# PSUM banks given out oldest free first instead of lowest free first

## The chip, the cores and the metric

The kernel runs on one core of one Trainium2 chip. The core has a matrix engine (TensorE, PE in the profile), a vector engine (DVE), a scalar engine (ACT), GpSimd (POOL) and a sync engine (SP) that issues the DMAs. Matmuls write to PSUM, which is handed out here as eight banks of 128 partitions by 512 float32; DVE and ACT read them out. The metric is the device time of one execution in microseconds (us).

## What is computed

Two stages follow each other, with four batches, twelve heads, 448 tokens and a head size of 64. The first is attention that mixes heads before and after the softmax, the second a feed-forward network with a low-rank mix of the tokens ahead of it:

```python
scores = scale * np.matmul(q, k.transpose(0, 1, 3, 2))
scores = np.einsum('bhij,hg->bgij', scores, w_pre)
scores = scores - np.max(scores, axis=-1, keepdims=True)
attn = np.exp(scores)
attn = attn / (np.sum(attn, axis=-1, keepdims=True) + 1e-09)
attn = np.einsum('bhij,hg->bgij', attn, w_post)
out = np.matmul(attn, v)                     # (4, 12, 448, 64)
x = out.transpose(0, 2, 1, 3).reshape(4, 448, 768)
h = x.transpose(0, 2, 1) @ U @ V             # U 448x32, V 32x448
u = x + h.transpose(0, 2, 1)
ch = np.maximum(u @ w_ch1, 0.0) @ w_ch2      # 768 -> 3072 -> 768
return u + ch
```

## The kernel before

The program is written as a list of steps with ranks (`plan.add`), and a planner (`Plan.order`, L146) walks a model of the engines' times and writes the steps down in the order in which they would start. Each engine then runs its own steps strictly in that order. A step that needs a PSUM bank (`bank`, through `plan.where`) takes it when the planner starts it, and the bank is free again when the planner's model has finished the last step that reads it. Which bank it gets is decided by `Plan.find` (L112) and kept by `Plan.take` (L131).

The eight banks are not eight tiles. They are four tiles of two banks each, `bank0` to `bank3`, and a step that needs one bank gets half of a tile:

```python
BANKS = [sb["ps"].tile([128, 2, 512], F32, f"bank{i}") for i in range(4)]

def bank(*s):
    w = plan.where[s]
    return BANKS[w[0] // 2] if len(w) == 2 else BANKS[w[0] // 2][:, w[0] % 2]
```

The waits between engines are derived from these tiles when the program is built: an instruction that reads or writes a tile waits for earlier accesses by other engines to the same tile, whichever half they touch. Banks 2p and 2p+1 are the halves of tile `bankp`.

In attention the steps `qk` (scores, matmuls of L390), `pre` (first head mix, L421) and `post` (second head mix, L454) take a whole tile each; `av` (L492) takes one half. They are read out by copies (L302 on ACT, L304 on DVE), by the maximum (DVE, L426) and by the exponential (ACT, L431).

From about 400 us on the banks are taken one at a time. `lr` is the low-rank mix (L665, L683, L696). `up` (L736) is the product with the first weight matrix: 18 matmuls of 448 columns for one block f of 128 hidden features (24 blocks) and one batch b; `hh` (ACT, L741) and `hl` (DVE, L745) read its bank and write relu in two float32r parts. `dn` (L756) is the product with the second matrix: for one batch and one of six output columns c it is 3 matmuls per block, nearly always for two blocks at once and so 6 matmuls; `ac` (DVE, L760) adds its bank to the accumulator `acc`. At most three banks are out for `up`, six for `dn`, four for `lr`. For two blocks f and four batches that is 8 `up` and 24 `dn`, 288 matmuls; this pattern repeats 12 times. Between them DVE, POOL and ACT turn the weights from 64-bit words to float32 pairs (L580 to L601, then L302, L306, L309).

`find` gives a step of `PAIRS` (`qk`, `pre`, `post`) the lowest free tile. A step that needs one bank gets the lowest bank whose other half is taken, or else the first half of the lowest free tile.

Of the kernel before, what the change touches and what calls it, by code (L numbers as in the profile page):

```python
# [43 lines left out]
class Unit:  # L44


    def __init__(self, b, gi):
        self.b, self.gi, self.n = b, gi, UNITS[b][gi]
        self.i0 = MC * sum(UNITS[b][:gi])
        self.rows = MC * self.n  # L50
        self.tokens = min(S, self.i0 + self.rows) - self.i0
# [11 lines left out]
PAIRS = ("qk", "pre", "post")  # L63
# [23 lines left out]
class Plan:  # L87
# [8 lines left out]
    def __init__(self, rings, banked, banks, weight):  # L96
        self.left = dict(rings)
        self.banked, self.where = banked, {}
        self.bank_free = [True] * banks
        self.weight = weight  # L100
        self.steps = {}
        self.port = {}
        self.users = {}
# [7 lines left out]

    def find(self, name, free):  # L112

        pairs = [p for p in range(len(free) // 2) if free[2 * p] and free[2 * p + 1]]
        if name in PAIRS:
            return [2 * pairs[0], 2 * pairs[0] + 1] if pairs else None
        odd = [i for i, f in enumerate(free) if f and not free[i ^ 1]]
        one = odd or [2 * p for p in pairs]
        return one[:1] or None

    def fits(self, names):
        free = list(self.bank_free)
        for n in sorted(names, key=lambda n: n not in PAIRS):
            got = self.find(n, free)
            if got is None:
                return False
            for g in got:
                free[g] = False
        return True

    def take(self, s):  # L131
        got = self.find(s[0], self.bank_free)
        for g in got:
            self.bank_free[g] = False
        self.where[s] = got

    def order(self):
# [3 lines left out]
        for k, s in steps.items():  # L141
            for n in s[3]:
                assert n in steps, (k, n)
                after.setdefault(n, []).append(k)
        held, left = set(), dict(self.left)
        free = {e: 0 for e in ("SP", "PE", "ACT", "DVE", "POOL", None)}  # L146
        ready = {e: [] for e in free}
        events, seq, now, wire, out, shared = [], 0, 0, 0, [], 0

        def push(k, t):  # L150
            nonlocal seq
            seq += 1
            heapq.heappush(events, (t, seq, k, False))
# [27 lines left out]
        while events:  # L181
            now = events[0][0]
            while events and events[0][0] <= now:
                _, n, k, done = heapq.heappop(events)
                if k is None:
                    continue
                if not done:
                    for e, _ in steps[k][0]:
                        r = ready[e]
                        item = (steps[k][2], n, k)  # L190
                        i = len(r)
                        while i and r[i - 1] > item:
                            i -= 1
                        r.insert(i, item)
                    continue
                for s in steps[k][4]:
                    users[s] -= 1
                    if users[s] == 0:
                        held.discard(s)
                        if s[0] in self.banked:  # L200
                            for g in self.where[s]:
                                self.bank_free[g] = True
                        left[s[0]] += 1
                for a in after.get(k, []):
                    wait[a] -= 1
                    if wait[a] == 0:
                        push(a, now + (self.PE_LATENCY - self.LATENCY if steps[a][0][0][0] == "PE" else 0))
            moved = True
            while moved:
                moved = False  # L210
                for e in free:
                    if free[e] > now:
                        continue
                    r = pick(e)
                    if r is None:
                        continue
                    k = r[2]
                    engines, fn, _, _, slots = steps[k]
                    for o, _ in engines:
                        ready[o].remove(r)  # L220
                    for s in sorted(slots, key=lambda s: s[0] not in PAIRS):
                        if s not in held:
                            held.add(s)
                            if s[0] in self.banked:
                                self.take(s)
                            left[s[0]] -= 1
                    cost = dict(engines)[e]
                    if e == "SP":
                        cost, bytes_time = cost
                    if e == "PE" and now - free[e] > 600:  # L230
                        cost += min(cost, 850)
                    if e in self.port[k]:
                        cost += max(0, shared - now)
                        shared = now + cost
                    out.append((k, e, now, now + cost))
                    seq += 1
                    if e is None:
                        late = 0
                    else:
                        free[e] = now + cost  # L240
                        late = self.PE_LATENCY if e == "PE" else self.LATENCY
                        if e == "SP":
                            wire = max(wire, now + cost + self.DMA_START) + bytes_time
                            late = wire + self.DMA_DONE - now - cost
                        heapq.heappush(events, (now + cost, seq, None, False))
                        seq += 1
                    heapq.heappush(events, (now + cost + late, seq, k, True))
                    moved = True
# [4 lines left out]
def build(tc, q2, kt, vj, wpre_in, wpost_in, u_in, v_in, ident, w1j, w2, out, show=None):  # L253
# [305 lines left out]
    def piece(key, src, n, p, rank, finish, slots, opened, cost, early=None):  # L559
# [61 lines left out]
        if early:  # L621
            plan.add((key, "put"), [("SP", (480, 900 * s))], put, r0, [(key, 4)], [first_tmp])
            plan.add((key, "take"), [("SP", (480, 900 * s))], take, rank - RANK["raw"], [(key, "put"), opened], [tmp])
# [183 lines left out]
    if show is not None:  # L807
        show.extend(order)
# [65 lines left out]
```

## Time and profile before

| what | value |
|---|---|
| time, median of 3 runs | 1421.88 us (1420.87 to 1424.16) |
| the profiled execution | 1414.63 us |
| its span, first to last instruction | 1412.8 us |
| PE busy | 1132.8 us (80%) |
| PE weight loads busy | 891.2 us (63%) |
| DVE busy | 706.5 us (50%) |
| ACT busy | 388.0 us (27%) |
| POOL busy | 255.6 us (18%) |
| mean granted TensorE clock | 0.978 |

A busy PE is not a PE at its peak: matmuls overlap, and one of 448 columns shows as 0.36 us while the next starts 0.20 us after it. Idle time of PE is time in which no matmul is in flight. The chain of waits is the work that ended last, followed backwards; a line of it names what the end of the program was waiting for at that time. The granted clock is 1.00 at 2.4 GHz and 0.50 at 1.2 GHz.

### The profile page before, as it was taken

What the parts mean: (1) busy time and instruction counts of PE and PEld (TensorE: products, weight loads), DVE (VectorE), ACT (ScalarE), POOL (GpSimd) and SP (SyncE); (2) the same over time, 40 slices, a digit from 0 to 9 for tenths busy, and PEclk for the clock granted to TensorE, in tenths of its full rate; (3) what the DMA queues carried; (4) which work ended last, traced back from release to release, by engine and by line L of the source; (5) the groups of instructions that cost most, each with busy time, mean ns of one, the idle gap of its engine ahead of it and who ended that gap; (6) DMA issues with size and microseconds to landing.
All of it is one profiled execution on the core that took longest, in us unless ns stands there. A gap on an engine that the chain in (4) does not pass through costs nothing.

```text
span 1412.8 us, 29240 instructions
## 1 busy us (share of the span) xinstructions
PE 1132.8 (80%) x12456; PEld 891.2 (63%) x12456; DVE 706.5 (50%) x1271; ACT 388.0 (27%) x817; POOL 255.6 (18%) x389
## 2 busy tenths in 40 slices
PE   3998998988867778777787878787878877777776
PEld 0565665665655667666666666666666666666665
DVE  0654554566666457545555454454554454444433
ACT  2766566766632222110111111110111110110000
POOL 2111111121323113211121111111121111112000
PEclk8999999999988999999999999999999999999999
DMA  7566555566551002111111111111111111111013
GB/s 241 181 199 181 163 174 169 178 187 194 176 162 34 0 23 63 50 45 45 45 45 34 34 45 34 34 45 45 45 45 34 34 45 34 34 45 45 1 46 111
DMA packets 68030, 118.18 MB, mean 84 GB/s; under 512 B 17804, under 2 KB 54108, under 8 KB 67420
## 3 DMA queue, kind: packets, MB, share of 16 engines
q1 hardware_dynamic: 67900, 116.31, 27.5%
q8 instruction: 98, 1.61, 0.5%
q14 instruction: 32, 0.26, 0.1%
HBM read 62.72 MB, written 12.28 MB: 53 GB/s over the span
## 4 chain that ended last, share of the span: by engine, by line
PE 71%; DVE 15%; issue 4%; ACT 4%; DMA 4%; SPq 1%; POOL 0%; DVEq 0%; ACTq 0%; POOLq 0%
PE bank L736 26%; PE bank L756 25%; DVE acc L760 7%; PE bank L492 5%; PE bank L454 5%; PE bank L421 4%; PE bank L390 4%; DMA t<-s 3%; DVE hl L745 3%; ACT hh L741 2%; PE bank L683 1%; DVE xl L309 1%; SPq L397 1%; ACT s L302 1%; DVE acc L699 1%
## 5 line engine op out<-in xcount | busy, mean ns | idle before, releaser
L756 PE MATMUL bank<-hh,w1l 128*128 128x448 f32 x576 | 226.1, 392 | 125.6 <-DVE acc L760 75.2
L760 DVE TENSOR_TENSOR acc<-acc,bank 128x448 f32<-128x448 f32 x300 | 181.5, 618 | 246.4 <-PE bank L756 126.1
L736 PE MATMUL bank<-uh,w0l 128*128 128x448 f32 x576 | 218.4, 379 | 64.7 <-DVE hl L745 31.1
L756 PEld LDWEIGHTS bank<-hh,w1l 128*128 128x128 f32 x576 | 108.1, 188 | 186.1 <-DVE acc L760 114.6
L741 ACT ACTIVATE hh<-bank 128x448 fp32r<-128x448 f32 x96 | 52.2, 544 | 622.2 <-PE bank L736 537.9
L736 PE MATMUL bank<-ul,w0h 128*128 128x448 f32 x576 | 211.0, 366 | 0.0
L736 PE MATMUL bank<-uh,w0h 128*128 128x448 f32 x576 | 210.7, 366 | 0.0
L756 PE MATMUL bank<-hh,w1h 128*128 128x448 f32 x576 | 210.6, 366 | 0.0
L756 PE MATMUL bank<-hl,w1h 128*128 128x448 f32 x576 | 210.4, 365 | 0.0
L601 POOL TENSOR_TENSOR a<-a,x 128x384 f32<-128x384 f32 (+2 forms) x99 | 99.9, 1009 | 462.4 <-DVE x L597 455.2
L736 PEld LDWEIGHTS bank<-uh,w0l 128*128 128x128 f32 x576 | 109.0, 189 | 97.3 <-DVE hl L745 37.7
L745 DVE SCALAR_TENSOR_TENSOR hl<-bank,hh 128x448 fp32r<-128x448 f32 x96 | 59.8, 622 | 217.2 <-ACT hh L741 210.1
L426 DVE TENSOR_REDUCE mx<-bank 128x2 f32<-128x896 f32 x90 | 97.6, 1086 | 112.7 <-PE bank L421 112.7
L454 PEld LDWEIGHTS bank<-wr,e 60*56 60x56 f32 (+1 forms) x5760 | 103.0, 133 | 66.6 <-issue 59.3
L454 PE MATMUL bank<-wr,e 60*56 60x60 f32 (+1 forms) x5760 | 107.9, 220 | 26.4 <-issue 22.8
L390 PE MATMUL bank<-k,q 64*60 64x448 f32 (+1 forms) x768 | 101.4, 580 | 24.8 <-ACT s L302 18.3
L431 ACT ACTIVATE e<-bank,mx 128x448 f32<-128x448 f32 x180 | 112.7, 636 | 21.2 <-DVE rc L438 13.4
L736 PEld LDWEIGHTS bank<-uh,w0h 128*128 128x128 f32 x576 | 108.9, 189 | 8.4
L736 PEld LDWEIGHTS bank<-ul,w0h 128*128 128x128 f32 x576 | 109.2, 190 | 7.4
L756 PEld LDWEIGHTS bank<-hh,w1h 128*128 128x128 f32 x576 | 108.2, 188 | 8.8
L756 PEld LDWEIGHTS bank<-hl,w1h 128*128 128x128 f32 x576 | 108.5, 188 | 6.5
L421 PE MATMUL bank<-t,wpre 64*64 64x448 f32 x720 | 92.0, 556 | 5.0 <-ACT e L431 1.7
(59 smaller groups left out, 1130.1 us busy)
## 6 DMA issues: line engine op xcount, KB each, us to landing
t<-s SPq DMA_DIRECT2D x192, 210.0 KB
kr<-in_w1j SPq DMA_DIRECT2D x48, 384.0 KB
kr<-in_w SPq DMA_DIRECT2D x48, 384.0 KB
q<-in_q SPq DMA_DIRECT2D x32, 186.0 KB
v<-in_vj SPq DMA_DIRECT2D x4, 1440.0 KB
acc<-xs SPq DMA_DIRECT2D x4, 1344.0 KB
out<-acc SPq DMA_DIRECT2D x24, 224.0 KB
xs<-x SPq DMA_DIRECT2D x10, 360.0 KB
```

The lines of the kernel that those rows point to most:

```text
L390: eng.matmul(o[at, i, :S], lhsT=q[d, p, at], rhs=k[d, p, :], start=True, stop=True)
L421: eng.matmul(o[64 * j:64 * j + 64, i, :S], lhsT=wpre[64 * i:min(64 * i + 64, QW)], rhs=tt[u % 2][64 * i:min(64 * i + 64, QW), n, :], start ...
L426: eng.tensor_reduce(out=mx, in_=T["pre", k][:, :, :S], axis=AX.X, op=ALU.max, negate=True)
L431: eng.activation(out=e[:, i], in_=T["pre", k][:, i, :S], func=ACTF.Exp, bias=T["mx", k][:, i:i + 1], accum_out=sm[:, i:i + 1])
L454: eng.matmul(d[:, jj * H:(jj + 1) * H, i], lhsT=e[64 * j:64 * j + HALF, i, j0:j0 + m], rhs=wr[64 * j:64 * j + HALF, i].rearrange("p (g m) ...
L492: eng.matmul(z[i * D:(i + 1) * D, c, :n], lhsT=v[:, p + c, i, jj, :], rhs=a[:, jj * H + 2 * (p + c) + i, :n], start=(jj == 0), stop=(jj == ...
L601: eng.tensor_tensor(out=f32(a), in0=f32(a), in1=f32(x), op=ALU.add)
L736: eng.matmul(ps, lhsT=w[:, c * 128:(c + 1) * 128], rhs=u[:, c, :], start=(i == 0), stop=(i == 3 * KC - 1))
L741: eng.activation(out=hh, in_=T["up", f, b], func=ACTF.Relu)
L745: eng.scalar_tensor_tensor(out=hl, in0=T.pop(("up", f, b)), scalar=0.0, in1=f32(T["hh", f, b]), op0=ALU.max, op1=ALU.subtract)
L756: eng.matmul(ps, lhsT=w[:, cut], rhs=h, start=(i == 0), stop=(i == len(todo) - 1))
L760: eng.tensor_tensor(out=dst, in0=dst, in1=T.pop(("dn", f, b, c)), op=ALU.add)
```

## The change

The list of free banks is now kept in the order in which banks came free (`bank_free` is a list of numbers; a freed bank is appended), and `find` gives out from its front. A step that needs a tile gets the one whose later-freed half came free first. A step that needs one bank gets a half whose other half is taken, oldest first, as long as steps that need whole tiles are still to come (`pairs_left`); after that it gets the oldest free bank, whichever tile it lies in.

```diff
--- before.py
+++ after.py
@@ -96,7 +96,8 @@
     def __init__(self, rings, banked, banks, weight):
         self.left = dict(rings)
         self.banked, self.where = banked, {}
-        self.bank_free = [True] * banks
+        self.bank_free = list(range(banks))
+        self.banks = banks
         self.weight = weight
         self.steps = {}
         self.port = {}
@@ -111,12 +112,16 @@
 
     def find(self, name, free):
 
-        pairs = [p for p in range(len(free) // 2) if free[2 * p] and free[2 * p + 1]]
+        pairs = [i for i in free if i ^ 1 in free]
         if name in PAIRS:
-            return [2 * pairs[0], 2 * pairs[0] + 1] if pairs else None
-        odd = [i for i, f in enumerate(free) if f and not free[i ^ 1]]
-        one = odd or [2 * p for p in pairs]
-        return one[:1] or None
+            if not pairs:
+                return None
+            p = min(range(self.banks // 2), key=lambda p: max(free.index(i) if i in free else 99 for i in (2 * p, 2 * p + 1)))
+            return [2 * p, 2 * p + 1]
+        odd = [i for i in free if i ^ 1 not in free]
+        if self.pairs_left and odd:
+            return odd[:1]
+        return free[:1] or None
 
     def fits(self, names):
         free = list(self.bank_free)
@@ -125,13 +130,15 @@
             if got is None:
                 return False
             for g in got:
-                free[g] = False
+                free.remove(g)
         return True
 
     def take(self, s):
         got = self.find(s[0], self.bank_free)
         for g in got:
-            self.bank_free[g] = False
+            self.bank_free.remove(g)
+        if s[0] in PAIRS:
+            self.pairs_left -= 1
         self.where[s] = got
 
     def order(self):
@@ -143,6 +150,7 @@
                 assert n in steps, (k, n)
                 after.setdefault(n, []).append(k)
         held, left = set(), dict(self.left)
+        self.pairs_left = sum(s[0] in PAIRS for s in self.users)
         free = {e: 0 for e in ("SP", "PE", "ACT", "DVE", "POOL", None)}
         ready = {e: [] for e in free}
         events, seq, now, wire, out, shared = [], 0, 0, 0, [], 0
@@ -198,8 +206,7 @@
                     if users[s] == 0:
                         held.discard(s)
                         if s[0] in self.banked:
-                            for g in self.where[s]:
-                                self.bank_free[g] = True
+                            self.bank_free += self.where[s]
                         left[s[0]] += 1
                 for a in after.get(k, []):
                     wait[a] -= 1
```

Built, the two programs have the same steps in the same order on every engine; what differs is the tile and half in which results stand, and through it the waits. Line numbers of the change are higher by 7 from `find` on (L736 is L743, L741 is L748, L745 is L752, L756 is L763, L760 is L767). In the rows below `bank0_1_58` to `bank3_4_61` are the four tiles; the half isn't shown.

PE, in the middle of six `dn` of batch b of two blocks (`hh_99` and `hh_107` are relu parts of the two), before:

```order
L756 MATMUL bank1_2_59<-hh_107_9799,w1h_27_9526 128x448
L756 MATMUL bank1_2_59<-hh_99_9627,w1l_26_9286 128x448 [waits DVE_49]
L756 MATMUL bank1_2_59<-hl_100_9629,w1h_25_9284 128x448
L756 MATMUL bank1_2_59<-hh_99_9627,w1h_25_9284 128x448
L756 MATMUL bank1_2_59<-hh_107_9799,w1l_28_9529 128x448 [waits Pool_49]
L756 MATMUL bank1_2_59<-hl_108_9804,w1h_27_9526 128x448
L756 MATMUL bank1_2_59<-hh_107_9799,w1h_27_9526 128x448
L756 MATMUL bank1_2_59<-hh_99_9627,w1l_26_9286 128x448 [waits DVE_49]
```

and in the change:

```order
L763 MATMUL bank0_1_58<-hh_107_9799,w1h_27_9526 128x448
L763 MATMUL bank2_3_60<-hh_99_9627,w1l_26_9286 128x448 [waits DVE_49]
L763 MATMUL bank2_3_60<-hl_100_9629,w1h_25_9284 128x448
L763 MATMUL bank2_3_60<-hh_99_9627,w1h_25_9284 128x448
L763 MATMUL bank2_3_60<-hh_107_9799,w1l_28_9529 128x448
L763 MATMUL bank2_3_60<-hl_108_9804,w1h_27_9526 128x448
L763 MATMUL bank2_3_60<-hh_107_9799,w1h_27_9526 128x448
L763 MATMUL bank0_1_58<-hh_99_9627,w1l_26_9286 128x448 [waits DVE_49]
```

Before, the `dn` of six matmuls stands in the tile of the `dn` just ahead of it, and its wait for DVE is for the addition of that one; in the change it stands in another tile, and its wait is for the addition of the last but one.

DVE around the same six `dn`, before:

```order
L745 SCALAR_TENSOR_TENSOR hl_110_9822<-bank0_1_58,hh_109_9820 128x448
L760 TENSOR_TENSOR acc_1_6295<-acc_1_6295,bank0_1_58 128x448
L760 TENSOR_TENSOR acc_1_6295<-acc_1_6295,bank1_2_59 128x448 x5
L745 SCALAR_TENSOR_TENSOR hl_112_9904<-bank1_2_59,hh_111_9899 128x448
L309 TENSOR_TENSOR w0l_32_9906<-a_66_9802,w0h_31_9901 128x384
L582 TENSOR_SCALAR x_67_9912<-kr_67_9824 128x384
L587 TENSOR_SCALAR a_82_9910<-kr_66_9806 128x384
L587 TENSOR_SCALAR a_68_9913<-kr_67_9824 128x384
```

and in the change:

```order
L752 SCALAR_TENSOR_TENSOR hl_110_9822<-bank3_4_61,hh_109_9820 128x448
L767 TENSOR_TENSOR acc_1_6295<-acc_1_6295,bank2_3_60 128x448
L767 TENSOR_TENSOR acc_1_6295<-acc_1_6295,bank0_1_58 128x448
L767 TENSOR_TENSOR acc_1_6295<-acc_1_6295,bank2_3_60 128x448
L767 TENSOR_TENSOR acc_1_6295<-acc_1_6295,bank0_1_58 128x448
L767 TENSOR_TENSOR acc_1_6295<-acc_1_6295,bank1_2_59 128x448
L767 TENSOR_TENSOR acc_1_6295<-acc_1_6295,bank3_4_61 128x448
L752 SCALAR_TENSOR_TENSOR hl_112_9904<-bank1_2_59,hh_111_9899 128x448
L316 TENSOR_TENSOR w0l_32_9906<-a_66_9802,w0h_31_9901 128x384
L589 TENSOR_SCALAR x_67_9912<-kr_67_9824 128x384
```

The order of the additions (`acc`) and of the weight conversions is the same; five additions in a row read `bank1` before, and now the tiles are `bank2`, `bank0`, `bank2`, `bank0`, `bank1`, `bank3`.

ACT, the reading of five `up` that follow each other on PE with `dn` between some of them (`hh` is the relu part; the CAST and the L580 rows belong to the weights), before:

```order
L741 ACTIVATE hh_105_9764<-bank0_1_58 128x448
L580 ACTIVATE x_79_9766<-kr_64_9735 128x384
L302 CAST w1h_29_9740<-a_64_9687 128x384
L741 ACTIVATE hh_107_9799<-bank0_1_58 128x448
L580 ACTIVATE x_65_9801<-kr_65_9771 128x384
L741 ACTIVATE hh_109_9820<-bank0_1_58 128x448
L741 ACTIVATE hh_111_9899<-bank1_2_59 128x448
L302 CAST w0h_31_9901<-a_66_9802 128x384
L580 ACTIVATE x_81_9909<-kr_66_9806 128x384
L741 ACTIVATE hh_113_9925<-bank1_2_59 128x448
```

and in the change:

```order
L748 ACTIVATE hh_105_9764<-bank3_4_61 128x448
L587 ACTIVATE x_79_9766<-kr_64_9735 128x384
L309 CAST w1h_29_9740<-a_64_9687 128x384
L748 ACTIVATE hh_107_9799<-bank1_2_59 128x448
L587 ACTIVATE x_65_9801<-kr_65_9771 128x384
L748 ACTIVATE hh_109_9820<-bank3_4_61 128x448
L748 ACTIVATE hh_111_9899<-bank1_2_59 128x448
L309 CAST w0h_31_9901<-a_66_9802 128x384
L587 ACTIVATE x_81_9909<-kr_66_9806 128x384
L748 ACTIVATE hh_113_9925<-bank3_4_61 128x448
```

The `up` whose results were in `bank0` three times running are now in `bank3`, `bank1`, `bank3`, `bank1` in turn, so that two that follow each other no longer share a tile.

## Rows read from the trace of the kernel before

**Rows 1.** Busy us by stretch: PE, PEld, DVE, ACT, POOL; granted clock, DMA, GB/s.

```profile
400.00:480.00 80.00, 55.55 (x263) 45.65 (x263) 48.26 (x87) 23.68 (x48) 20.39 (x20) 0.85 0.21 63
...
600.00:1330.00 730.00, 580.34 (x2648) 484.50 (x2649) 358.95 (x701) 93.87 (x191) 131.63 (x138) 1.00 0.14 39
```

**Rows 2.** Chain of waits, start, length, work: two pattern starts, one long piece.

```profile
721.24 3.66 PE bank L736 x18
...
800.40 3.66 PE bank L736 x18
...
836.25 8.80 PE bank L756 x42
```

**Rows 3.** Who waited for whom, whole span: total us, times, longest us.

```profile
PE bank L756 <- DVE acc L760: 75.2, 103, 1.0
...
PE bank L756 <- DVE hl L745: 47.2, 37, 1.4
...
PE bank L736 <- DVE hl L745: 31.1, 23, 2.0
...
PE bank L736 <- DVE acc L760: 24.5, 34, 0.9
...
PE bank L736 <- POOL w0h L306: 7.3, 9, 0.8
```

**Rows 4.** Timeline around a `dn` that waits for an addition: start, length, instruction.

```profile
977.13 0.37 PE L756 MATMUL bank<-hh,w1h 128*128 128x448 f32 x1
977.54 0.62 DVE L760 TENSOR_TENSOR acc<-acc,bank 128x448 f32<-128x448 f32 x1 [0.44 <-PE bank L756]
978.22 0.47 PE L756 MATMUL bank<-hh,w1l 128*128 128x448 f32 x1 [0.71 <-DVE acc L760]
978.52 0.36 PE L756 MATMUL bank<-hl,w1h 128*128 128x448 f32 x1
```

**Rows 5.** Timeline around a `dn` that waits for `hl`, after an `up`.

```profile
971.93 0.36 PE L736 MATMUL bank<-uh,w0h 128*128 128x448 f32 x1
972.33 0.54 ACT L741 ACTIVATE hh<-bank 128x448 fp32r<-128x448 f32 x1 [3.77 <-PE bank L736]
...
972.90 0.62 DVE L745 SCALAR_TENSOR_TENSOR hl<-bank,hh 128x448 fp32r<-128x448 f32 x1 [1.20 <-ACT hh L741]
...
973.58 0.47 PE L756 MATMUL bank<-hh,w1l 128*128 128x448 f32 x1 [1.29 <-DVE hl L745]
```

**Rows 6.** Timeline of DVE, instructions that follow each other without a wait.

```profile
997.47 0.61 DVE L760 TENSOR_TENSOR acc<-acc,bank 128x448 f32<-128x448 f32 x1
998.00 0.35 DVE L596 TENSOR_SCALAR x<-a 128x384 int32<-128x384 int32 x1
998.39 0.56 DVE L597 SCALAR_TENSOR_TENSOR x<-kr,x 128x384 f32<-128x384 uint32 x1
998.87 1.15 DVE L760 TENSOR_TENSOR acc<-acc,bank 128x448 f32<-128x448 f32 x2
```

**Rows 7.** Timeline, a POOL and a DVE instruction at the same time.

```profile
968.63 1.01 POOL L309 TENSOR_TENSOR w1l<-a,w1h 128x384 fp32r<-128x384 f32 x1 [2.31 <-ACT w1h L302]
968.67 1.38 DVE L591 SCALAR_TENSOR_TENSOR a<-kr,a 128x384 int32<-128x384 int32 x1
```

**Rows 8.** One line's instructions from 700 to 1200 us: shortest, median, longest ns.

```profile
L591 DVE SCALAR_TENSOR_TENSOR a<-kr,a x50: 550/552/1391, 701.1 to 1193.4; 128x384 int32<-128x384 int32 x50
```

**Rows 9.** Granted clock in one us, columns as in rows 1.

```profile
450.00:451.00 1.00, 1.00 (x4) 0.87 (x4) 0.00 (x0) 0.00 (x0) 0.00 (x0) 0.50 0.00 0
```

**Rows 10.** Timeline of PE in that us: matmuls of an `up`.

```profile
450.13 0.57 PE L736 MATMUL bank<-uh,w0h 128*128 128x448 f32 x1
450.51 0.57 PE L736 MATMUL bank<-uh,w0l 128*128 128x448 f32 x1
```

**Rows 11.** PE's waits from 27 to 480 us: total us, times, longest us.

```profile
PE bank L683 <- DVE xl L309: 8.1, 4, 2.6
PE bank L390 <- ACT s L302: 3.8, 4, 1.3
```

## The prediction

> **What bounds the kernel now.** I read four views in this order. First the busy time by stretch: from 600 to 1330 us, half of the span, PE is busy 580 of 730 us at a granted clock of 1.00, DVE 359, ACT 94, POOL 132 [rows 1]. PE is the engine with most to do there, but it is not saturated, and nothing else is near its limit. Second the chain of waits, which shows the pattern of two blocks and four batches repeating: it starts at 721.24 and again at 800.40, so it takes 79.16 us [rows 2]. Eighteen undisturbed matmuls take 3.66 us, 0.203 us each [rows 2]; the 288 of a pattern would take 58.5 us. So 20.7 us of each pattern are stops, and 12 patterns make 248 us. Third, who PE waits for: additions `acc` and relu parts `hl`, both on DVE, and nine times a name on POOL [rows 3]. Fourth the timeline around one stop of each kind. Behind a `dn`, PE's last matmul starts at 977.13, DVE adds at 977.54 and PE starts again at 978.22 [rows 4]. The two engines take turns: the new `dn` writes into the half tile next to the one that is being added, and the tile is what is waited for. Behind an `up` the same happens with `hh` and `hl` in between: 971.93 to 973.58 [rows 5].
>
> **The price of one stop.** An undisturbed pair of matmul starts lies 0.203 us apart. Across a stop for an addition the two steps take 1.09 and 0.30 us, 0.98 more than 0.41, while the profile shows 0.71 idle [rows 4]: the idle time leaves out 0.16 us in which the last matmul still drains and 0.10 us by which the first one afterwards is slower. For `hl` the same sum is 1.65 + 0.30 - 0.41 = 1.54, with 1.29 shown [rows 5]. So each stop costs its idle time and about 0.27 us more.
>
> **What goes.** Added up, rows 3 hold 75.2 + 47.2 + 31.1 + 24.5 + 7.3 = 185.3 us of idle time in 103 + 37 + 23 + 34 + 9 = 206 stops. With 0.27 us each that is 185.3 + 55.6 = 240.9 us, against the 248 of the pattern's sum. The nine stops under POOL's name belong here: in the built program those `up` wait for a POOL conversion that is long done and for an addition in their own tile.
>
> In the built order each of PE's waits can be followed to the matmul whose result the awaited DVE instruction reads, and the matmuls between that one and the waiting one counted. Before, 189 waits of `up` and `dn` have none in between. In the change none is left: 116 waits for an addition have six, that is one whole `dn`, and 76 waits for an addition or `hl` have eighteen, one whole `up`; about ten lie elsewhere, most at the start and the end of the stretch. An addition needs 1.09 - 0.20 = 0.89 us from the end of the last matmul's slot [rows 4], and a `dn` in between gives 6 x 0.203 = 1.22: 0.33 us to spare. A `hl` needs 1.65 - 0.20 = 1.45 us [rows 5], an `up` gives 3.66: 2.2 us to spare. That a wait which is already met costs nothing is to be seen before as well: the 42 matmuls at 836.25, seven `dn`, some of them with waits that are met by then, take 8.80 us, 0.21 each [rows 2]. So I take all 240.9 us as gone.
>
> **What comes back or stays.** *Late additions.* DVE runs its list in order, and in 49 of the 116 cases two conversion instructions stand between an addition and the one before it. Two additions with L596 and L597 between them start 1.40 us apart [rows 6], 0.18 more than a `dn` takes; one such is covered by the 0.33 us, two close together are not. Going by hand through one pattern of 24 `dn` with these durations, I find two stops of 0.2 to 0.3 us, with 0.1 each for the slower first matmul: 0.7 to 1.0 us per pattern. I take 12 us for 12 patterns; the bounds are 0 and 116 x 0.5 = 58 us, every one of them late by about the two conversions and a restart.
>
> *True waits.* At the end of the program a `dn` follows its own `hl` with little in between, and the bank makes no difference there. I leave 5 us of the 240.9 in place (0 to 10).
>
> *The low-rank mix.* From 400 to 480 us PE is busy 55.6 of 80 us [rows 1], much of it in waits for data, as the 8.1 us for `xl` [rows 11]. Waits with less than one us of matmul work behind the release fall there from 25 to 9 in the built order. I take 5 us as gained (0 to 20).
>
> *Attention.* Its tiles also change places, but waits with less than one us behind the release are 85 before and 84 now. What PE waits there for banks is small (the largest is 3.8 us [rows 11], all together about 12 us). I take 0, from -8 to +8.
>
> *Everything else.* No instruction is added or taken away, and every engine's list has the same order. Weight loads, additions and conversions run beside the matmuls as before. What is late next is PE's own work: 3456 matmuls of 0.203 us, 702 us, plus attention.
>
> Sum: 1414.6 (the profiled execution) - 240.9 + 12 + 5 - 5 = 1185.7 us. The median of the runs shown lies 7.3 us above the profiled execution, so the predicted time is 1193 us.
>
> **Rivals.** *DVE becomes the late one (10%).* For it: the conversions of a pattern now fall into 60 us where they had 79, DVE's 359 of 730 us become about two thirds of the time, and an instruction of DVE can last 1.38 us instead of 0.55 when a POOL instruction runs at the same time [rows 7]; its longest is 1391 ns with a median of 552 [rows 8]. Against: the median says that this is rare. Price: the upper bound of 58 us instead of 12, 1239 us. The Trainium skill, "SBUF — State Buffer", section "Who interferes with whom", says that a DVE instruction with two inputs from SBUF and a POOL instruction that reads SBUF shut each other out for a whole instruction. The trace agrees, with 1.38 us where 0.55 is usual [rows 7, 8]; by the page alone every overlap costs this much and the sum goes to this rival's, by the rows it is a few per pattern.
>
> *Weights become late (6%).* PE comes to a new block sooner, and POOL can write its `w0h` and `w0l` only when the last `up` of an older block is done. Price: with POOL's 1.0 us for a low part [rows 7], half of that for the high part and the restart, about 1.9 us for each of 24 blocks, 45 us: 1238 us. Against: the built order puts these conversions 144 matmuls, 29 us, ahead of the `up` that needs them.
>
> *The clock (2%), the case that ends slower.* At a granted clock of 0.50 [rows 9] matmuls start 0.38 us apart [rows 10], 0.177 more than at 1.00. If PE's clock fell to 1.2 GHz again and again in the long stretch, the 229 us gained would be used up once 1290 of its 3456 matmuls ran so; with half of them the time would be 1193 + 1728 x 0.177 = 1499 us. Against: the clock is 1.00 there although PE stops some 17 times per pattern [rows 1, 3], and now it stops less. The Trainium skill, "TensorE: Matmul & The Clock Gate", section "A second HAM failure mode: psum-queue depth-cycling", reports a kernel whose cycling through banks with short idle times between groups made the clock go up and down. This kernel's trace disagrees: its stops left the clock at 1.00. By that rule the time would be this rival's, by the row there is no loss.
>
> *It doesn't do what it says (2%).* If the waits stayed between neighbouring halves, the time would stay at 1422 us. The built order speaks against it: `dn` that follow each other stand in different tiles.
>
> **How the numbers follow.** My forecast, 1193 us, has 80%. Its own range goes from 1193 - 12 - 15 = 1166 (no late addition, all of the low-rank gain) to 1193 + 46 + 8 = 1247 (all additions late, attention's loss), and both middle rivals end inside it; I give 1165 to 1245. A measurement of this kernel can tell about 0.2% from no change. Faster than that: 0.96; within it: 0.02; slower: 0.02, the clock.
>
> **What would show it.** The pattern should take 59 to 61 us instead of 79.16. PE's waits for `acc` and `hl` should fall from 178 us to under 20, those left should be short and sit behind two conversions. PE's busy share from 600 us on should rise from 80% to well over 90%, the clock stay at 1.00, and attention end at about the same time. I am wrong if the pattern stays above 65 us, if another releaser, above all POOL or a DMA, takes the place of `acc`, or if the clock drops in the long stretch.

## The result: 18% faster, a little more than the range allowed

| | before | after |
|---|---|---|
| median | 1423.02 us (1420.87 to 1427.24, 4 runs) | 1162.12 us (1158.00 to 1164.86, 4 runs) |
| profiled execution, its span, its mean clock | 1414.63, 1412.8, 0.978 | 1160.33, 1158.2, 0.979 |

The ratio is 0.8161, 95% interval [0.8127, 0.8195]. The forecast was 1193 us, the range 1165 to 1245: the direction and the price of the stops held, the gain was some 30 us larger than forecast, and the range missed by 3 us. Which of two waits makes a stop was read wrongly (below).

In the kernel after the change, line numbers are 7 higher than before: `up` is L743, `hh` L748, `hl` L752, `dn` L763, `acc` L767, the low-rank steps `tp`, `t1`, `hp` are L672, L690, L703.

Busy time by stretch of the kernel after (stretch, length, then PE, PEld, DVE, ACT, POOL with instruction counts, granted clock, DMA share, GB/s), the answer to the second line of [rows 1]:

```profile
600.00:1100.00 500.00, 499.89 (x2409) 450.14 (x2408) 345.78 (x635) 86.66 (x174) 121.40 (x125) 1.00 0.18 51
```

PE had 580 busy of 730 us; now it has 499.89 of 500, at the same clock of 1.00. DVE's share went from 49% to 69% by getting the same work done in less time.

The chain of waits of the kernel after (start, length, work), the answer to [rows 2]:

```profile
657.12 7.38 PE bank L743 x36
664.50 15.31 PE bank L763 x72
679.82 11.15 PE bank L743 x54
...
716.99 7.43 PE bank L743 x36
...
776.98 3.09 PE bank L743 x15
```

A pattern runs from 657.12 to 716.99 and from there to 776.98: 59.87 and 59.99 us, against 79.16. The chain holds nothing but PE: ACT and DVE no longer appear in it here.

PE's waits of the kernel after from 500 us to the end (us, times, longest), the answer to [rows 3]; it is the whole answer:

```profile
PE bank L763 <- DVE hl L752: 0.5, 1, 0.5
```

And the same for weight loads over the whole span, where a late addition still shows, since the matmul before it is still draining:

```profile
PEld bank L763 <- DVE acc L767: 9.7, 30, 0.4
```

The timeline of the kernel after, at one of these late additions (start, length, instruction, idle before it and who ended it), beside [rows 4]:

```profile
676.26 0.62 DVE L767 TENSOR_TENSOR acc<-acc,bank 128x448 f32<-128x448 f32 x1
...
676.62 0.37 PE L763 MATMUL bank<-hh,w1h 128*128 128x448 f32 x1
...
676.93 0.19 PEld L763 LDWEIGHTS bank<-hh,w1l 128*128 128x128 f32 x1 [0.32 <-DVE acc L767]
676.93 0.47 PE L763 MATMUL bank<-hh,w1l 128*128 128x448 f32 x1
...
677.24 0.36 PE L763 MATMUL bank<-hl,w1h 128*128 128x448 f32 x1
```

Here DVE did two conversions before the addition, and PE starts at 676.93 instead of 676.82. Both steps take 0.31 where 0.20 is undisturbed: 0.2 us lost where [rows 4] lost 0.98.

**Where the 254.6 us of span came from.** On every engine the sequence of instructions is the same before and after, so the same instruction can be looked up in both traces. I cut both at the first and the last matmul of the low-rank steps:

| | before | after | gain | forecast |
|---|---|---|---|---|
| attention, up to the first low-rank matmul | 386.6 | 378.4 | 8.2 | 0 |
| the low-rank stretch, first to last matmul | 119.2 | 96.5 | 22.7 | 5 |
| everything behind it | 907.1 | 683.3 | 223.8 | 223.9 |

Behind the stretch, in steps from one matmul of `up` or `dn` to the next: before, 203 steps lay over 0.6 us and cost 215.2 us more than an undisturbed one; one is left, with 0.7 us. Steps of 0.25 to 0.6 us fell from 213 (23.1 us) to 62 (7.1 us). All other steps became slower, from 202.4 to 205.1 ns in the mean, which is about 8.5 us on the 3212 of them in the change.

**Which wait was the false one.** The section on the change says that before, a waiting `dn` waits for the addition of the `dn` just ahead of it, and the prediction that it writes next to the half that is being added. Both are wrong. Followed in the built program, the `dn` that starts at 978.22 in [rows 4] writes the very half that the addition at 977.54 reads. What this addition reads is the result of the last `dn` but one, whose last matmul starts here (timeline of the kernel before):

```profile
975.92 0.36 PE L756 MATMUL bank<-hh,w1h 128*128 128x448 f32 x1
```

So PE's wait is a true one. The false one is the addition's own: its row shows 0.44 us of idle time that ended with PE, because DVE had to let the `dn` in the other half end first, whose last matmul is the one at 977.13. In [rows 5] it is the same with `hh`: it reads an `up` whose last matmul starts at 966.71,

```profile
966.71 0.36 PE L736 MATMUL bank<-uh,w0h 128*128 128x448 f32 x1
```

and is held for the `up` in the other half, to 972.33. Of the 203 stops 188 are of this kind, 132 at an addition and 56 at an `hl`, with 199.4 of the 215.2 us; in 14 PE itself waits for a reader of the other half. By the built program 184 of the 282 additions behind the low-rank stretch and all 90 `hh` wait for a matmul in the other half before, and 8 additions and no `hh` in the change. There it is the other way about: PE waits for the addition in the neighbouring half, in 116 cases with six matmuls in between.

### The profile page after: what moved, and what is told of

Its sections match the earlier page's. It is cut to its first block, busy times and chain, and to the rows that moved or that the text cites. A ratio compares the mean times of both kernels' runs of the same rounds, so it can differ in the third digit from the quotient of the medians.

```text
span 1158.2 us, 29292 instructions
## 1 busy us (share of the span) xinstructions
PE 1086.0 (94%) x12456; PEld 902.0 (78%) x12456; DVE 730.3 (63%) x1271; ACT 390.5 (34%) x817; POOL 258.4 (22%) x389
## 4 chain that ended last, share of the span: by engine, by line
PE 83%; DMA 7%; DVE 5%; issue 2%; ACT 2%; SPq 1%; POOL 0%; ACTq 0%; DVEq 0%; POOLq 0%
PE bank L743 30%; PE bank L763 29%; PE bank L461 6%; PE bank L499 6%; DMA t<-s 5%; PE bank L428 5%; PE bank L397 5%; PE bank L690 1%; DVE acc L767 1%; DMA v<-in_vj 1%; PE bank L672 1%; SPq L404 1%; DVE xl L316 1%; ACT s L309 1%; DVE a L599 1%
## 5 line engine op out<-in xcount | busy, mean ns | idle before, releaser
L767 DVE TENSOR_TENSOR acc<-acc,bank 128x448 f32<-128x448 f32 x300 | 183.9, 619 | 76.2 <-PE bank L763 71.2
L763 PE MATMUL bank<-hh,w1l 128*128 128x448 f32 x576 | 215.2, 374 | 1.7 <-DVE xl L316 0.6
L743 PE MATMUL bank<-uh,w0l 128*128 128x448 f32 x576 | 213.0, 370 | 0.9 <-DVE acc L706 0.7
L743 PE MATMUL bank<-ul,w0h 128*128 128x448 f32 x576 | 212.5, 369 | 0.0
L743 PE MATMUL bank<-uh,w0h 128*128 128x448 f32 x576 | 212.3, 369 | 0.0
L763 PE MATMUL bank<-hl,w1h 128*128 128x448 f32 x576 | 211.4, 367 | 0.0
L763 PE MATMUL bank<-hh,w1h 128*128 128x448 f32 x576 | 211.4, 367 | 0.0
L748 ACT ACTIVATE hh<-bank 128x448 fp32r<-128x448 f32 x96 | 52.3, 545 | 396.2 <-PE bank L743 364.1
L752 DVE SCALAR_TENSOR_TENSOR hl<-bank,hh 128x448 fp32r<-128x448 f32 x96 | 59.8, 623 | 133.2 <-ACT hh L748 132.1
L763 PEld LDWEIGHTS bank<-hh,w1l 128*128 128x128 f32 x576 | 108.3, 188 | 22.0 <-DVE acc L767 9.7
L743 PEld LDWEIGHTS bank<-uh,w0l 128*128 128x128 f32 x576 | 109.1, 189 | 11.6 <-DVE acc L706 1.0
L743 PEld LDWEIGHTS bank<-uh,w0h 128*128 128x128 f32 x576 | 108.9, 189 | 10.1
L743 PEld LDWEIGHTS bank<-ul,w0h 128*128 128x128 f32 x576 | 108.9, 189 | 9.9
L763 PEld LDWEIGHTS bank<-hh,w1h 128*128 128x128 f32 x576 | 108.3, 188 | 9.7
L763 PEld LDWEIGHTS bank<-hl,w1h 128*128 128x128 f32 x576 | 108.3, 188 | 9.0
## 6 DMA issues: line engine op xcount, KB each, us to landing
kr<-in_w1j SPq DMA_DIRECT2D x48, 384.0 KB
kr<-in_w SPq DMA_DIRECT2D x48, 384.0 KB
```

The costliest lines, as they stand in the source:

```text
L743: eng.matmul(ps, lhsT=w[:, c * 128:(c + 1) * 128], rhs=u[:, c, :], start=(i == 0), stop=(i == 3 * KC - 1))
L748: eng.activation(out=hh, in_=T["up", f, b], func=ACTF.Relu)
L752: eng.scalar_tensor_tensor(out=hl, in0=T.pop(("up", f, b)), scalar=0.0, in1=f32(T["hh", f, b]), op0=ALU.max, op1=ALU.subtract)
L763: eng.matmul(ps, lhsT=w[:, cut], rhs=h, start=(i == 0), stop=(i == len(todo) - 1))
L767: eng.tensor_tensor(out=dst, in0=dst, in1=T.pop(("dn", f, b, c)), op=ALU.add)
```

## The experiments

All are compared with the kernel before on the same chip. "Stops" are steps of over 0.6 us between matmuls of `up` or `dn` behind the low-rank stretch, counted in the trace.

**Is it the age, or the shared tile?** (e3, e4) Both keep the new rule in attention. e3 gives out the oldest bank, but always fills a half-used tile first; e4 forgets age once attention's pairs are out and takes the lowest bank of a wholly free tile.

```
e3:  -        if self.pairs_left and odd:
     -            return odd[:1]
     -        return free[:1] or None
     +        return (odd or free)[:1] or None
e4:  +        if not self.pairs_left:
     +            low = sorted(free)
     +            return ([i for i in low if i ^ 1 in low] or low)[:1] or None
```

> Free banks are kept oldest first as in the change, but a step that needs one bank always gets a half whose other half is taken, if there is one, to the end of the program. Theory (the stops come from two steps that share a tile): 198 waits of up and dn have no matmul in between, against 189 before and none in the change, so the time is that of before, 1415 to 1435 us, and the pattern of two blocks takes about 79 us. Rival (what costs is that the bank given out has only just come free): the age rule alone brings the gain, 1160 to 1200 us.

> Attention as in the change; afterwards the lowest free bank again, as before, but first one whose tile is wholly free. Theory (shared tiles): no wait is left without a matmul in between, though banks are given out again as soon as they come free; 1155 to 1175 us, pattern about 60 us. Rival (age of the bank): lowest first brings the stops back, 1350 to 1425 us.

e3: 1405.0 us (1403.55 to 1406.23), ratio 0.9894 [0.9855, 0.9932], 200 stops. e4: 1147.72 us (1142.34 to 1151.28), ratio 0.8074 [0.8028, 0.8121], no stop. PE's waits of e3 over the whole span, to be laid beside [rows 3]:

```profile
PE bank L760 <- DVE acc L764: 65.4, 91, 1.4
PE bank L760 <- DVE hl L749: 45.8, 36, 1.4
PE bank L740 <- DVE hl L749: 31.1, 23, 1.9
PE bank L740 <- DVE acc L764: 30.0, 42, 0.8
```

The waits of before are all there, in the oldest banks there are; in 198 of the 200 stops a reader is again held by the neighbour's matmul. Age without a change of tile gives 1%; a change of tile without age gives all of the gain and 14 us more than the change. e3 came out 10 us below its expectation's low end, e4 7 us below its own.

**Is any of it in attention?** (e1, e2) e1 uses the old rule while whole tiles are still to come, and the new one after that; e2 is the reverse.

```
e1:  +        if self.pairs_left:
     +            low = sorted(free)
     +            (the old rule on low)
e2:  the same behind "if not self.pairs_left:"
```

> The old rule as long as steps that need whole tiles are still to come, the new one after that: attention has its banks of before. If the 8 us by which attention ended earlier in the changed kernel come from the banks, 1168 to 1173 us and the first low-rank matmul at about 386 us; if they are chance (stops of PE under the name issue), 1160 to 1165 us.

> The new rule as long as steps that need whole tiles are still to come, the old one after that. Theory: the feed-forward stretch has its 189 waits without a matmul in between again, so nearly all of the gain is gone: 1412 to 1425 us, 1415 if attention's 8 us belong to the banks and 1423 if not. Rival (the gain is in attention's tiles): under 1300 us.

e1: 1163.21 us, ratio 0.8195 [0.8161, 0.8229]: the change's time. e2: 1417.26 us, 0.9971 [0.995, 0.9992], with the 203 stops of before. The banks in attention give at most 0.5%.

**Whose banks make the low-rank stretch long?** (e5, e6) Here the forecast was off by most. e5 is the change with the low-rank steps alone under the old rule, e6 is before with them alone under the new one.

```
e5:  +        if name == "lr":
     +            (the old rule)
e6:  +        if name != "lr":
     +            (the old rule)
```

> The change, with the low-rank steps (tp, t1, hp) alone given their bank by the rule of before: a half-used tile first, then the lowest free one. All other work keeps the new rule. Reads in the low-rank stretch that wait for a matmul in the other half of their tile go from 29 to 39 by the built program, the matmul work so waited for from 20.0 to 29.4 us (before: 43 reads, 49.4 us); behind the stretch 12 stops of a dn for hl are left, at 1.54 us some 18 us. Theory (the stretch is long or short by how many reads of ACT and DVE wait for a neighbour's matmul): the stretch from the first to the last low-rank matmul takes 100 to 106 us, between the change's 96.5 and before's 119.2, and the time is 1178 to 1192 us. Rival 1 (only PE's own bank waits count there, as the prediction took it): the stretch stays at 94 to 99 us and the time is 1174 to 1182. Rival 2 (the low-rank steps' own banks are the whole of it): the stretch takes 116 to 122 us, the time is 1195 to 1205.

> The kernel before, with the low-rank steps alone given the oldest free bank by the new rule. By the built program 41 reads in the stretch wait for a neighbour's matmul, with 47.8 us of matmul work (before: 43 and 49.4), and 188 stops without work in between are left behind it (before 189). Theory (the neighbours' matmuls decide): the stretch takes 114 to 120 us as before, and the time is 1405 to 1425 us. Rival (the low-rank steps' own banks decide): the stretch takes 95 to 100 us and the time is 1385 to 1402.

e5: 1196.42 us (1195.66 to 1197.75), 0.8412 [0.8383, 0.8442]; e6: 1402.87 us (1392.9 to 1409.26), 0.9856 [0.9804, 0.9909]. Busy time in the low-rank stretch of before, of the change, of e5 and of e6 (columns as above; the fences are in this order):

```profile
386.60:505.80 119.20, 84.90 (x562) 70.63 (x556) 68.36 (x122) 35.43 (x70) 26.53 (x28) 0.90 0.21 62
```

```profile
378.40:474.90 96.50, 79.83 (x561) 70.18 (x556) 69.32 (x122) 35.40 (x70) 26.38 (x28) 0.91 0.26 77
```

```profile
383.70:490.40 106.70, 83.06 (x558) 72.31 (x556) 69.06 (x122) 35.36 (x70) 26.98 (x28) 0.89 0.24 70
```

```profile
387.10:493.50 106.40, 83.86 (x557) 72.24 (x556) 68.89 (x121) 35.43 (x70) 26.82 (x28) 0.90 0.24 70
```

Either half of the change alone takes 12.5 or 12.8 us from the stretch, both together 22.7. So the steps' own banks and their neighbours' count for about half each, as far as one execution of each can tell (the second one of before has 124.2 us instead of 119.2). For e5 the theory's 100 to 106 is nearly met and both rivals fall; the time is above its range, because behind the stretch 36 stops of 24.6 us stood instead of 12 of 18, with 77 short ones of 12.3 us. For e6 both expectations missed: it lies between them, though the built program has almost as many reads that wait for a neighbour's matmul as before. Such a count is too coarse.

The trace tells more than the count. ACT's waits in the stretch of before (`t` is the copy of a `t1` result, which L683 makes; `hh` reads an `up`, L736):

```profile
ACT hh L741 <- PE bank L683: 12.1, 2, 6.0
...
ACT hh L741 <- PE bank L696: 8.7, 3, 4.9
ACT t L302 <- PE bank L736: 7.2, 1, 7.2
...
ACT t L302 <- PE bank L665: 5.0, 3, 2.2
```

and DVE's, where `xl` reads a `tp` (L665):

```profile
DVE xl L309 <- PE bank L736: 3.4, 1, 3.4
```

All of these wait for a matmul whose result they don't read: in the built program it stands in the other half of their tile. The 7.2 us lie around the us of [rows 9, 10], at half clock, where the 18 matmuls of an `up` take 18 x 0.38 = 6.8 us; the 3.4 us are nearly the 3.66 of an `up` at full clock [rows 2]. While the reader waits, the next low-rank matmul has no data, and PE's wait is put down to that data. In the kernel after, ACT's waits of these two kinds for a foreign step are

```profile
ACT hh L748 <- PE bank L703: 8.7, 2, 4.8
...
ACT t L309 <- PE bank L672: 7.0, 4, 3.0
```

and `hh` and `t` wait for their own steps otherwise. Added up over ACT and DVE (`t`, `xh`, `xl`, `hh`, `hl`, `acc`), the idle time that ended with another step's matmul goes with the length of the stretch. The last column is worked out from the built program: the idle time of the same readers that ended with a matmul in the other half of their tile, whichever step it is of:

| run | stretch, us | idle for another step's matmul, us | idle for a matmul in the other half, us |
|---|---|---|---|
| before again | 124.2 | 60.1 | 68.0 |
| e2 | 122.6 | 59.3 | 67.4 |
| before | 119.2 | 54.0 | 62.0 |
| e3 | 115.9 | 55.5 | 56.6 |
| e5 | 106.7 | 32.1 | 34.7 |
| e6 | 106.4 | 22.5 | 33.7 |
| change again | 97.5 | 22.1 | 24.3 |
| change | 96.5 | 22.0 | 24.1 |
| e1 | 96.0 | 15.7 | 17.9 |
| e4 | 92.7 | 8.4 | 9.1 |
| e9 | 88.8 | 4.0 | 4.1 |

By the third column e6 would be as short as the change. It is 10 us longer, 4 us of them in matmul time (83.86 against 79.83 busy) and 6 in PE's own stops. The last column has the reason: e6's readers also wait for the neighbour's matmuls of the same step in another batch, and so it stands beside e5, not beside the change. That column falls with the stretch throughout (e8 and e10, with extra DVE work in the stretch, have 98.7 us with 22.9 and 93.3 with 4.1, so it is not all that counts); that the one makes the other is supported by e5 and e6, but no run changed a reader's wait alone.

The stretch also runs at a granted clock below 1.00, and some of its gain is matmul time: PE's busy time fell by 5.1 us (84.90 to 79.83), its idle time by 17.6 (34.3 to 16.7).

**How much room has DVE?** (e8) The change, with one more copy behind each addition.

```
         eng.tensor_tensor(out=dst, in0=dst, in1=T.pop(("dn", f, b, c)), op=ALU.add)
+        eng.tensor_copy(out=sb["extra"], in_=dst[:, :224])
```

> The change, with one more DVE instruction behind each of the 300 additions: a copy of 128x224 elements of the sum into a tile that nobody reads. It is extra work, of about 0.2 to 0.3 us each (an estimate from the additions of 448 elements, 0.55 us), 60 to 90 us of DVE in all. Theory (DVE has margin; an addition is late only where conversions stand close together): in some 49 of 116 places with one dn in between the addition comes up to 0.3 us later, 15 us at most; the time is 1165 to 1180 us, and the short stops of 0.25 to 0.6 us between matmuls go from 62 to 70 to 120. Rival (DVE is nearly the bound in the long stretch): half or more of DVE's extra time shows, 1195 to 1250 us.

1213.60 us (1208.84 to 1216.86), 0.8529 [0.8497, 0.8562]: 51 us more than the change, with 34 stops. The time is the rival's, its reason holds in part. In e8's groups of instructions (busy us, mean ns | idle before) the copies are dearer than I had estimated,

```profile
L769 DVE COPY extra<-acc 128x224 f32<-128x224 f32 x300 | 110.3, 368 | 10.3
```

and of their 110 us 47% came out. The mean hides two kinds of copy (this line's instructions: shortest, median, longest ns; first and last start):

```profile
L769 DVE COPY extra<-acc x300: 276/277/1082, 418.3 to 1204.1; 128x224 f32<-128x224 f32 x150
```

Of the 300 copies 244 take under 0.3 us and 56 take 0.46 to 1.08; every one of the 56 overlaps an instruction of POOL in the trace, of the 244 only 11 do. PE's waits from 500 us on:

```profile
PE bank L764 <- DVE acc L768: 33.0, 41, 1.3
```

DVE has 387 of 500 us to do from 600 on, some 77%. Its timeline shows one of the long copies:

```profile
689.29 0.61 DVE L768 TENSOR_TENSOR acc<-acc,bank 128x448 f32<-128x448 f32 x1
689.94 0.72 DVE L769 COPY extra<-acc 128x224 f32<-128x224 f32 x1
690.58 0.61 DVE L768 TENSOR_TENSOR acc<-acc,bank 128x448 f32<-128x448 f32 x1
```

From one addition to the next are 1.29 us here, and a `dn` takes 1.22. That is not the rule: of 82 such pairs with nothing but a copy in between the median is 0.84 us, and 27 lie above 1.22. Of PE's waits with six matmuls in between, 1 of 36 came late where the copy alone stands ahead of the awaited addition, 39 of 49 where two conversions stand there with it, and 10 of 21 where an `hl` does. So DVE has room in the mean, and none where its list is dense.

**Both rules together, and the same load on it** (e9, e10). e9 takes, once attention's pairs are out, the oldest bank whose tile is wholly free. By the built program nearly every wait then has 12 or more matmuls behind it, where the change has 116 with six. (e4 has 106 additions with six, but only nine of them behind two conversions, against 49 in the change; none came late.) e10 is e9 with e8's copies.

```
e9:  +        if not self.pairs_left:
     +            return ([i for i in free if i ^ 1 in free] or free)[:1] or None
```

> The change, but once the last pair of banks has been given out, a single bank is the oldest free one whose tile is wholly free, and only if there is none the oldest of all. By the built program no wait of up or dn stands directly behind its neighbour, and nearly all have 12 or more matmuls in between (the change: 116 with six); in the low-rank stretch 8 reads wait for a neighbour, with 9.9 us of matmul work (the change 29 and 20.0; the rule with the lowest wholly free tile 10 and 16.3). Theory (sharing of a tile and the distance to it are all that counts): at most 11 short stops, a low-rank stretch of 86 to 92 us, 1138 to 1148 us in all, at or a little below the 1147.7 of the lowest wholly free tile. Rival (the gain of that one was chance, in the spacing of the undisturbed matmuls): the time is 1153 to 1163 us.

> The oldest bank of a wholly free tile first, as in the run before it, with the same extra DVE copy of 128x224 elements behind each of the 300 additions, 0.37 us each by that run, 110 us in all. In the change this copy cost 51 us, with 34 stops of over 0.6 us. Theory (there the copies were felt because PE wants the neighbouring half again after one dn, six matmuls; here 12 or more lie between, and DVE's sum of work still fits): at most 8 stops of over 0.6 us and 1148 to 1165 us. Rival (DVE has no room for another 110 us wherever the banks are): 30 or more such stops and 1185 to 1205 us.

e9: 1147.87 us (1146.26 to 1149.51), 0.8070 [0.8045, 0.8094], no stop, one short one, and the shortest low-rank stretch:

```profile
387.20:476.00 88.80, 76.41 (x558) 68.27 (x556) 68.06 (x121) 35.78 (x70) 27.54 (x28) 0.94 0.29 84
```

e4 and e9 can't be told apart, and both beat the change, whose interval lies above theirs. e9 is the version that I would keep, for what e10 shows: 1177.73 us (1168.43 to 1178.82), 0.8291 [0.8251, 0.8331]. The same copies cost 30 us on e9 and 51 on the change; on e4 they were not tried. Both expectations for e10 missed: the distance takes up part of DVE's delay, but not all. Its profiled execution, at 1168.43 us the fastest of five, has 10 stops, nine of them at additions with twelve matmuls in between that stand behind a copy and two conversions. PE's waits of e10 from 480 us on:

```profile
PE bank L765 <- DVE acc L769: 12.0, 9, 1.4
```

**What differs from one execution to the next?** The change and the kernel before, once more, unaltered.

> The change once more, unaltered, for a second profile. If attention's 8 us less and the spacing of undisturbed matmuls (202 or 206.5 ns, by turns) differ from one execution to the next: the first low-rank matmul starts anywhere from 378 to 388 us, more than 1 us from the 378.4 of the first profile, and the mean spacing is not 205.1 ns again but anywhere from 202.5 to 206. If they belong to the program: 378 to 379 us and 205 ns. In both cases the low-rank stretch takes 94 to 99 us and one stop of over 0.6 us is left behind it.

> The kernel before once more, unaltered, for a second profile. If attention's length differs from one execution to the next, its first low-rank matmul starts anywhere from 380 to 390 us; if it belongs to the program, at 386 to 387 us. The low-rank stretch takes 116 to 123 us, with 203 stops of over 0.6 us behind it.

Change again: 1161.59 us; first low-rank matmul at 378.8, stretch 97.5, 1 stop, 69 short ones. Before again: 1420.94 us; 385.7, 124.2 (one us over what I expected), 203 stops. So each gave its own time of attention again, within 1 us. But it doesn't belong to the banks. e2, e3, e4, e5, e8, e9, e10 and the change run the same instructions in the same banks up to there, and reach it at 385.7, 385.8, 384.0, 383.7, 381.9, 387.2, 375.0 and 378.4. With the old banks (before, e1, e6) it is 386.6, 383.0 and 387.1. The spread of 12 us among equal programs is larger than the 8 us to be explained, and they are up to 8 us apart at the hundredth matmul, where PE has done little but wait for its first data. Two executions of each are too few to say that it belongs to the program: e10's runs lie 10 us apart, and its profiled one, the fastest, has the earliest start of all, 375.0. What sets it stays open.

## Where the prediction held and where it failed, step by step

- **The price of a stop and their count: right.** 206 stops with 240.9 us were to go. Behind the low-rank stretch alone, long and short stops held 215.2 + 23.1 = 238.3 us and hold 0.7 + 7.1 now.
- **Which wait makes a stop: wrong, at no cost to the sum.** I had PE's wait for the neighbouring half as the false one. In 188 of 203 stops it was the reader's wait ahead of it, for the matmuls in the neighbouring half; the result that it read was six or eighteen matmuls old, and not of the matmul just ahead. PE and the reader take turns either way, so count and price came out right. But the same reading left out the reader's side where it did matter, in the low-rank mix.
- **No new wait takes their place: right.** Nothing but one `hl` of 0.5 us is left from 500 us on; no weight, no DMA. PE does 499.89 us of work in 500.
- **Late additions: 12 forecast, 7 measured.** Their kind was right: of the 49 additions behind two conversions 29 came late, and nearly all of the 62 short stops are theirs, two to each, about 0.24 us an addition. My two per pattern were 24. Their price was too high: two of 0.2 to 0.3 with 0.1 each for the restart are 0.6 to 0.8 us per pattern and 7 to 10 us in all, not the 0.7 to 1.0 and 12 of the prediction. The upper bound of 58 us was far off.
- **True waits: 5 forecast, 0.7 measured.**
- **The unforeseen 8.5 us.** With these two terms some 9 us too high, the part behind the stretch should have come out lower than forecast. It didn't, since undisturbed matmuls became 2.7 ns slower (below). The agreement of 223.8 with 223.9 is in part two errors that cancel.
- **The low-rank mix: the step that failed.** 5 forecast with 20 as a bound, 22.7 measured. I took PE's waits for `xl` [rows 11] as waits for data that a bank can't shorten, and counted only PE's own waits for a half tile. But the reader can be held as well: the copy that makes the data waits for a matmul in the other half of its source. These waits stood in the trace of before, in ACT's and DVE's lines, which the prediction doesn't use. Sized by them (54.0 us of such idle time) the bound would have been 50 and not 20.
- **Attention: 0 forecast, 8.2 measured,** just beyond the ±8. The reason, that the banks give nothing there, holds by e1 and e2; the cause of the 8.2 us is open.
- **The range.** Its low end let the late additions go to nothing and the low-rank stretch to its bound, but not attention to its own at the same time. Two of the three passed their bounds together.
- **From the profiled execution to the median: 7.3 us added, 1.8 measured** (1162.12 less 1160.33). With the 17.7 us of the low-rank mix and the 8.2 of attention, these 5.5 make up the 31 us between forecast and measurement; they are the spread of single executions, and no gain of the change.

The rivals: weights did not become late, and the tiles did change. The clock stayed at 1.00 with stops and without. The Trainium skill, "TensorE: Matmul & The Clock Gate", section "A second HAM failure mode: psum-queue depth-cycling", would have it fall where banks are cycled with short idle times; the traces of the long stretch here disagree, for 203 stops as for none. DVE being late was the rival nearest to the truth: it cost 7 us in the change, and e8 shows that 0.37 us more per addition in the mean bring it about, with 51 us.

## What to carry to other kernels

Where a tile spans two banks and dependences are kept by tile, "which bank is free" is the wrong question: give out a bank whose tile is wholly free, and age comes second (e3 against e4). Look for the false wait on both sides: the writer that waits for the neighbour's reader shows as a wait of PE, the reader that waits for the neighbour's writer hides behind a wait "for data" or behind a true wait of PE for its own half, and is found by asking, for each reader, whether the matmul that it waits for is the one whose result it reads. Here nearly all stops of the long stretch were of the second kind. And once PE is full, count the distance in matmuls from release to reuse: in the change six were enough for every addition with none or one conversion ahead of it, and too few for 29 of the 49 behind two.

## What the runs showed of the hardware that I had not expected

Undisturbed matmuls of equal shape at a granted clock of 1.00 don't all have the same spacing. In the change three `up`, 54 matmuls, took 11.15 us at the same place of two successive patterns (chain of waits, start, length, work):

```profile
698.40 11.15 PE bank L743 x54
...
758.39 11.15 PE bank L743 x54
```

In the second execution of the same program the same pieces took less:

```profile
702.55 10.90 PE bank L743 x54
...
762.07 10.90 PE bank L743 x54
```

and so they did in e9:

```profile
696.89 10.90 PE bank L744 x54
...
755.35 10.90 PE bank L744 x54
```

That is 206.5 against 201.9 ns. Either holds for some us to tens of us, and no bank has it to itself (means by bank in the change lie between 204.8 and 206.0 ns). From 600 us on the slower spacing (a mean of over 204.2 ns over 18 undisturbed steps) has 77% of the change and 56% of its second execution, 2% and 17% of before's, 15% of e4's and e9's. It costs the change some 7 us against e4 and e9, about half of what they gain on it; the rest of their gain is the 62 short stops and the shorter low-rank stretch, less a later start of that stretch. In e4 and e9 it doesn't come by chance: it is at the same two of the eight `up` in every pattern. No run here tells what sets the spacing.
